# Half of k of batch 0 in fp32 from SyncE's queue, and three reorderings that go with it

## The chip, the cores and the metric

One core of one Trainium2 chip runs the whole program. The metric is the device time of one execution in microseconds (us), as the median of several executions. The profile's span, from the first to the last instruction, is about 1.75 us shorter than that time, so spans and times are not mixed below. Engines are called PE (TensorE), DVE (VectorE), ACT (ScalarE), POOL (GpSimd) and SP (SyncE).

## The reference

Linear attention in 8 batches of 8 heads, and then a gated feed-forward block on its output:

```python
def phi(x): return np.where(x > 0, x, np.exp(x) - 1.0) + 1.0     # = min(exp x, 1) + max(x, 0)
q_p, k_p = phi(q), phi(k)                       # q, k, v: [8, 8, 576, 64], fp32
kv  = einsum('bhsd,bhse->bhde', k_p, v)
z   = sum(k_p, axis=2)
num = einsum('bhsd,bhde->bhse', q_p, kv)
den = einsum('bhsd,bhd->bhs', q_p, z) + 1e-6
x   = (num / den) -> [4608, 512]
g   = x @ w_gate                                # [512, 1536]
out = (g * sigmoid(g) * (x @ w_val)) @ w_out    # [1536, 512]
```

## The kernel before

Tokens go through in 9 groups of 512. Layer 1 (`w_gate`, `w_val`, 12 blocks of columns) and layer 2 (`w_out`) are long matmuls of 512 columns in fp16, 216 ns each. Attention for the next batches is done in between, in short matmuls. Batch 0 and most of batch 1 are special: nothing precedes them that could hide their work. So for them q is transposed on PE, the denominators are made on PE ("corners" with Zr), and ACT takes 1/den as exp(-ln(den)).

All loads but one go through POOL's queue and are cast from fp32 to fp16 on the way. Half of q of batch 0 comes in fp32 from SP's queue and is cast by DVE:

```python
WARM = (34, 14, 16, 7, 3, 3, 2)        # dummy matmuls that keep PE busy during waits
...
nc.sync.dma_start(out=q32[:, :, :], in_=q[0]...[:, 0:2, :])
ld(q, qr, 0, 1)                        # cast load, second half of q of batch 0
ld2(k, kr, 0)                          # cast loads, both halves of k
ld(v, vr, 0, 0)
...
for l in range(2):
    nc.vector.tensor_copy(out=qr[0][:, l, :], in_=q32[:, l, :])
warm(WARM[0])
for lp in range(2):
    qtr(0, lp, pq[lp])                 # 16 transposes of q on PE
    warm(WARM[1 + lp])
    ph[lp][0]()                        # ACT: exp of q
exp_k(0, 0)                            # ACT: exp of k
exp_k(0, 1)
...
```

In layer 2 of group 0, the denominators of batch 1's tokens (`s4`) start at block 7 of 12, and `kv_corner(1, ...)` later writes k.v of batch 1 into the pair of PSUM banks `dz`:

```python
def lnrd(ps, i, w0=0, w1=512):
    for l2 in range(2):
        act(lnt[2 * i + l2][:, w0:w1], ps[l2][:, w0:w1], AF.Ln, bias=epsb[:, 0:1])
        act(rd[i][:, l2, w0:w1], lnt[2 * i + l2][:, w0:w1], AF.Exp, scale=-1.0)
...
step = {1: [s0], 3: [s1, s3], 7: [s4]}
FO = 8
for fb in range(FO):
    for f in step.get(fb, []): f()
    for t in range(4): l2_mm(0, t, fb)
for t in range(4):
    if t == 2:
        for lp in range(2): kv_corner(1, lp, kp, True, True)     # into dz
        r_copy(1, 0, 2, "VV")
    if t == 3: nx(0, dz)
    for fb in range(FO, FB): l2_mm(0, t, fb)
    if t < 3: l2_out(0, t, "V")
nx(1, cq)
```

In layer 2 of group 1, `block(1)` runs k.v of batches 2 and 3 (2 x 72 short matmuls) and 24 corner matmuls in one go.

## Time and profile before

| before | value |
|---|---|
| time, median (range) | 316.58 us (316.45 to 316.88, 4 executions) |
| span of the profiled execution | 315.4 us |
| PE busy | 309.3 us, 98% |
| first layer-1 matmul after blocks 0 and 1 (A) | 20.99 us |
| from A to the same point of group 1 (B) | 35.12 us |
| from B to the first layer-1 matmul of group 2 (C) | 30.21 us |
| from C to the end | 229.06 us |

The last four rows are read from the timeline of PE. They cut the span into four stretches: a change in the start shows in A, in layer 2 of group 0 in A to B, in the block of batch 2 in B to C.

The profile's chain of work that ended last (start us, duration us, what):

```profile
0.74 3.61 DMA q<-in_q_dram
...
4.38 1.14 DVE qr L425 x2
...
6.62 1.61 PE pp L122 x14
8.23 1.02 PE pp L368 x9
9.24 0.02 issue
9.27 1.02 ACT qT L118
10.29 1.06 ACT ek L118
11.35 0.02 issue
11.37 0.47 DVE ek L145
...
18.42 2.74 PE pp L274 x12
21.16 17.27 PE pp L290 x80
```

Up to 21 us several engines take turns, and L122 is dummy work. From there it is PE alone: 80 matmuls in 17.27 us, 216 ns each. Only the start has room. Note that the exp of k (ek) comes after the second exp of q (qT), which waits for a transpose of the second half of q.

The same start by windows (us, busy time of each engine with the number of its instructions, granted clock, DMA share, GB/s moved):

```profile
0.00:4.00 4.00, 2.94 (x28) 2.95 (x29) 0.89 (x7) 1.28 (x1) 2.87 (x9) 1.00 0.49 155
4.00:8.00 4.00, 3.62 (x39) 2.96 (x36) 1.42 (x3) 1.02 (x1) 3.50 (x6) 1.00 1.10 154
8.00:12.00 4.00, 3.83 (x55) 3.17 (x53) 2.78 (x6) 2.73 (x3) 2.18 (x3) 1.00 1.26 199
```

The bytes are counted as written, so a cast load counts half of what it reads. Between 4 and 8 us the queues move 154 GB/s, under the 199 of the next window: a hint that I did not use when I predicted. (The figure after the busy times is the granted clock. The view prints 1.00 there also where the trace has no clock record.)

Later, ACT and PE in layer 2 of group 0:

```profile
46.47 0.69 ACT L118 ACTIVATE lnt<-pp,epsb 128x512 f32<-128x512 f32 x1 [2.77 <-PE pp L252]
47.19 0.63 ACT L118 ACTIVATE rd<-lnt 128x512 f16<-128x512 f32 x1
47.72 0.67 ACT L118 ACTIVATE lnt<-pp,epsb 128x512 f32<-128x512 f32 x1
...
49.28 0.80 PE L183 MATMUL pp<-vr,kp 64*64 64x64 f16 x72
```

The second Ln ends at 48.39 us, and k.v of batch 1 starts 0.9 us later, at 49.28.

### The profile page before, as it was taken

What the parts mean: (1) busy time and instruction counts of PE and PEld (TensorE: products, weight loads), DVE (VectorE), ACT (ScalarE), POOL (GpSimd) and SP (SyncE); (2) the same over time, 40 slices, a digit from 0 to 9 for tenths busy, and PEclk for the clock granted to TensorE, in tenths of its full rate; (3) what the DMA queues carried; (4) which work ended last, traced back from release to release, by engine and by line L of the source; (5) the groups of instructions that cost most, each with busy time, mean ns of one, the idle gap of its engine ahead of it and who ended that gap; (6) DMA issues with size and microseconds to landing.
All of it is one profiled execution on the core that took longest, in us unless ns stands there. A gap on an engine that the chain in (4) does not pass through costs nothing.

```text
span 315.4 us, 5768 instructions
## 1 busy us (share of the span) xinstructions
PE 309.3 (98%) x2311; PEld 148.5 (47%) x2311; DVE 204.5 (65%) x354; ACT 151.2 (48%) x228; POOL 48.3 (15%) x73
## 2 busy tenths in 40 slices
PE   8999999999999999999999999999999999999994
PEld 7744444444544454445444544445444444444442
DVE  2754867999689676978598749874991434134410
ACT  2765849638653655357434743475331333133311
POOL 7655344300000230014000500000000000000000
PEclk9999999999999999999999999999999999999999
DMA  7999999997612297129803890314022400140014
GB/s 154 198 198 199 206 207 225 244 207 106 139 33 41 48 166 183 30 47 148 213 4 72 125 236 1 76 30 105 2 53 59 98 1 1 35 100 0 0 35 100
DMA packets 41163, 32.52 MB, mean 103 GB/s; under 512 B 16432, under 2 KB 36400, under 8 KB 41136
## 3 DMA queue, kind: packets, MB, share of 16 engines
q0 software_dynamic: 20736, 18.58, 37.9%
q1 hardware_dynamic: 20320, 13.54, 18.4%
q8 instruction: 18, 0.29, 0.4%
q14 instruction: 9, 0.07, 0.1%
q10 hardware_dynamic: 80, 0.03, 0.0%
HBM read 37.75 MB, written 9.44 MB: 150 GB/s over the span
## 4 chain that ended last, share of the span: by engine, by line
PE 96%; DMA 1%; DVE 1%; ACT 1%; issue 0%; DVEq 0%
PE pp L290 57%; PE pp L297 30%; PE pp L274 2%; PE pp L252 2%; PE pp L183 2%; DMA q<-in_q_dram 1%; PE pp L368 1%; PE pp L122 1%; DVE qr L425 0%; ACT ek L118 0%; ACT qT L118 0%; PE pp L393 0%; DVE xT L406 0%; PE pp L210 0%; DVE osb L320 0%
## 5 line engine op out<-in xcount | busy, mean ns | idle before, releaser
L118 ACT ACTIVATE sil<-pp 128x512 f16<-128x512 f32 x108 | 63.4, 597 | 102.0 <-PE pp L290 94.3
L290 PE MATMUL pp<-xT,wg 128*128 128x512 f16 x416 | 106.8, 379 | 0.0
L290 PE MATMUL pp<-xT,wv 128*128 128x512 f16 x416 | 106.8, 379 | 0.0
L283 DVE SCALAR_TENSOR_TENSOR hT<-pp,sil 128x512 f16<-128x512 f32 x108 | 72.2, 680 | 46.8 <-PE pp L290 34.9
L297 PE MATMUL pp<-wo,hT 128*128 128x512 f16 (+2 forms) x444 | 97.0, 374 | 0.6 <-DVE osb L320 0.6
L297 PEld LDWEIGHTS <-hT 128*128 128x128 f16 x444 | 41.9, 98 | 49.9 <-issue 2.1
L290 PEld LDWEIGHTS <-wv 128*128 128x128 f16 x416 | 40.6, 98 | 49.2
L290 PEld LDWEIGHTS <-wg 128*128 128x128 f16 x416 | 40.6, 98 | 48.5
L320 DVE TENSOR_SCALAR osb<-pp 128x512 f32<-128x512 f32 (+1 forms) x19 | 12.9, 681 | 32.7 <-PE pp L297 32.7
L118 ACT ACTIVATE osb<-pp 128x512 f32<-128x512 f32 (+1 forms) x18 | 10.2, 572 | 34.3 <-PE pp L297 34.3
L118 ACT ACT_TABLE_LOAD x13 | 16.7, 1283 | 2.3 <-PE pp L290 2.1
L118 ACT ACTIVATE ek<-kr 128x1152 f16<-128x1152 f16 x16 | 17.7, 1154 | 0.1
L657 POOL COPY gate<-qT 128x1 f16<-128x1 f16 x4 | 1.2, 305 | 97.9 <-DMA qT<-qp 70.2
L227 DVE TENSOR_TENSOR qp<-qp,rden 128x1152 f16<-128x1152 f16 x12 | 16.2, 1347 | 0.0
L218 DVE TENSOR_REDUCE den<-prod 128x18 f32<-128x1152 f16 x12 | 16.1, 1342 | 0.0
L269 DVE TENSOR_SCALAR xT<-pp 128x512 f16<-128x512 f32 (+1 forms) x14 | 8.8, 666 | 7.7 <-PE pp L252 7.7
L118 ACT ACTIVATE eq<-qr 128x1152 f16<-128x1152 f16 x12 | 13.2, 1147 | 0.0
L101 POOL DMA_DIRECT2D vr<-in_v_dram x16 | 11.7, 734 | 8.3 <-PE pp L290 3.1
L101 POOL DMA_DIRECT2D kr<-in_k_dram x16 | 11.5, 722 | 8.1 <-DMA vr<-in_v_dram 3.6
L101 POOL DMA_DIRECT2D qr<-in_q_dram x15 | 11.0, 734 | 7.2 <-DMA wo<-in_moe_w_out_dram 1.8
L145 DVE TENSOR_SCALAR ek<-ek 128x1152 f16<-128x1152 f16 x16 | 8.1, 508 | 5.7 <-ACT ek L118 5.7
L157 DVE TENSOR_TENSOR kp<-ek,kp 128x1152 f16<-128x1152 f16 x14 | 10.6, 758 | 0.5
(68 smaller groups left out, 189.5 us busy)
## 6 DMA issues: line engine op xcount, KB each, us to landing
out_dram<-osb SPq DMA_DIRECT2D x70, 128.0 KB, 3.7
kr<-in_k_dram POOLq DMA_DIRECT2D x16, 288.0 KB, 8.6
vr<-in_v_dram POOLq DMA_DIRECT2D x16, 288.0 KB, 9.9
qr<-in_q_dram POOLq DMA_DIRECT2D x15, 288.0 KB, 11.7
wo<-in_moe_w_out_dram POOLq DMA_DIRECT2D x3, 512.0 KB, 13.0
wg<-in_moe_w_gate_dram POOLq DMA_DIRECT2D x5, 256.0 KB, 9.7
wv<-in_moe_w_val_dram POOLq DMA_DIRECT2D x5, 256.0 KB, 10.3
q<-in_q_dram SPq DMA_DIRECT2D x1, 576.0 KB, 3.6
```

The costliest lines, as they stand in the source:

```text
L101: nc.gpsimd.dma_start(out=dst[b % NB][:, 2 * lp:2 * lp + 2, :], in_=src[b].rearrange("(l a) (c j) d -> (a c) l (j d)", a=2, j=J)[:, 2 * lp ...
L118: nc.scalar.activation(out=out, in_=in_, func=func, bias=bias, scale=scale)
L145: nc.vector.tensor_scalar(out=a, in0=a, scalar1=1.0, scalar2=None, op0=ALU.min)
L157: nc.vector.tensor_tensor(out=a, in0=ek[b % 2][:, lp, :, :], in1=a, op=ALU.add)
L183: nc.tensor.matmul(out=ps[hh][D * l2:D * l2 + D, D * lp:D * lp + D], lhsT=t[b % 2][rows, lp, j, D * l2:D * l2 + D], rhs=vr[b % NB][rows, 2 ...
L218: nc.vector.tensor_reduce(out=den[:, c, :], in_=prod[:, :, :].rearrange("p j (l d) -> p (j l) d", d=D), axis=AX.X, op=ALU.add)
L227: nc.vector.tensor_tensor(out=qv, in0=qv, in1=rden[:, c, :].unsqueeze(2).to_broadcast([P, 2 * J, D]), op=ALU.mult)
L269: nc.vector.tensor_scalar(out=dst, in0=ps[l2][:, c0:], scalar1=1.0 / SC, scalar2=None, op0=ALU.mult)
L283: nc.vector.scalar_tensor_tensor(out=hT[g % 2][:, fb, :], in0=ps[1][:, :], scalar=SC, in1=s[:, :], op0=ALU.mult, op1=ALU.mult)
L290: nc.tensor.matmul(out=ps[h][:, :], lhsT=w[:, c, P * fb:P * fb + P], rhs=xT[g % 2][:, c, :], start=(c == 0), stop=(c == 3))
L297: nc.tensor.matmul(out=l2p[(g, t)][:, n0:n1], lhsT=hT[g % 2][:, fb, P * t:P * t + P], rhs=wo[:, fb, n0:n1], start=(fb == 0), stop=(fb == F ...
L320: nc.vector.tensor_scalar(out=o[:, n0:n1], in0=ps[:, n0:n1], scalar1=1.0 / SC, scalar2=None, op0=ALU.mult)
```

## The change

It is meant to shorten the start: k's first half also comes in fp32 from SP, so it arrives without queueing behind q on POOL's queue, and its exp can run in ACT's gap between the two exps of q. One of the two casts of q moves to ACT. To relieve group 0, the second half of batch 1's k is processed later, and layer 2 of group 0 is laid out anew for that (FO 9, the denominators after the loop). k.v of batch 2 gets a place of its own. The dummies are cut. The core of the diff:

```diff
-    WARM = (34, 14, 16, 7, 3, 3, 2)
+    WARM = (32, 8, 8, 6, 3, 3)
@@ loads
-    nc.sync.dma_start(out=q32[:, :, :], in_=q[0]...)
+    for (src, dst) in ((q, q32), (k, k32)):
+        nc.sync.dma_start(out=dst[:, :, :], in_=src[0]...)
     ld(q, qr, 0, 1)
-    ld2(k, kr, 0)
-    ld(v, vr, 0, 0)
+    ld(k, kr, 0, 1)
+    ld2(v, vr, 0)
     ... (batch 1's k: its halves one and two weight loads later)
@@ batch 0
-    for l in range(2):
-        nc.vector.tensor_copy(out=qr[0][:, l, :], in_=q32[:, l, :])
+    nc.vector.tensor_copy(out=qr[0][:, 0, :], in_=q32[:, 0, :])
+    act(qr[0][:, 1, :], q32[:, 1, :])
     warm(WARM[0])
+    qtr(0, 0, pq[0])
+    ph[0][0]()
+    act(jl(ek, 0, 0), k32v, AF.Exp)
+    nc.vector.tensor_scalar(out=jl(kp, 0, 0), in0=k32v, scalar1=0.0, scalar2=None, op0=ALU.max)
     ... (cut: the same pieces of batch 0 in a new order)
@@ block(g), for batch 2
-            kv_all(b1)
-            r_copy(b1, 0, 2, "AA")
             kv_all(b2)
@@ layer2_0
-        step = {1: [s0], 3: [s1, s3], 7: [s4]}
-        FO = 8
+        step = {1: [s0], 4: [s1, s3], 5: [s5]}     # s0: now also batch 1's second k; s5: z
+        FO = 9
         for fb in range(FO):
             ...
+        s4()
@@ layer 2 of group 1
+                if t == 1 and g == 1:
+                    kv_all(b1)
+                    r_copy(b1, 0, 2, "AA")
```

More of the change, by code (lines that the diff above doesn't have):

```diff
@@ L65 @@
     q32 = sb.tile([P, 2, J * D], FP32, name="q32")
+    k32 = sb.tile([P, 2, J * D], FP32, name="k32")
     lnt = many([P, 512], FP32, "lnt", 4)
@@ L199, in r_copy, with zsum @@
                 nc.vector.tensor_copy(out=R[b % 3][:, l0:l1, hh, :], in_=src)
-    def zsum(b):
-        a = kp[b % 2]
-        nc.vector.tensor_tensor(out=zs[:, :, 0:4, :], in0=a[:, :, 0:4, :], in1=a[:, :, 4:8, :], op=ALU.add)
-        nc.vector.tensor_tensor(out=zs[:, :, 0:2, :], in0=zs[:, :, 0:2, :], in1=zs[:, :, 2:4, :], op=ALU.add)
-        nc.vector.tensor_tensor(out=zs[:, :, 0, :], in0=zs[:, :, 0, :], in1=zs[:, :, 1, :], op=ALU.add)
-        nc.vector.tensor_tensor(out=zs[:, :, 0, :], in0=zs[:, :, 0, :], in1=a[:, :, 8, :], op=ALU.add)
+    def zsum(b, l0=0, l1=2):
+        a, z = kp[b % 2][:, l0:l1, :, :], zs[:, l0:l1, :, :]
+        nc.vector.tensor_tensor(out=z[:, :, 0:4, :], in0=a[:, :, 0:4, :], in1=a[:, :, 4:8, :], op=ALU.add)
+        nc.vector.tensor_tensor(out=z[:, :, 0:2, :], in0=z[:, :, 0:2, :], in1=z[:, :, 2:4, :], op=ALU.add)
+        nc.vector.tensor_tensor(out=z[:, :, 0, :], in0=z[:, :, 0, :], in1=z[:, :, 1, :], op=ALU.add)
+        nc.vector.tensor_tensor(out=z[:, :, 0, :], in0=z[:, :, 0, :], in1=a[:, :, 8, :], op=ALU.add)
     def zb(b):
@@ L326, in l2_out @@
         return o
-    nc.sync.dma_start(out=q32[:, :, :],
-                      in_=q[0].rearrange("(l a) (c j) d -> (a c) l (j d)", a=2, j=J)[:, 0:2, :])
+    for (src, dst) in ((q, q32), (k, k32)):
+        nc.sync.dma_start(out=dst[:, :, :],
+                          in_=src[0].rearrange("(l a) (c j) d -> (a c) l (j d)", a=2, j=J)[:, 0:2, :])
     ld(q, qr, 0, 1)
     nc.gpsimd.iota(out=idx[:, :], pattern=[[-1, P]], base=0, channel_multiplier=1)
-    ld2(k, kr, 0)
-    ld(v, vr, 0, 0)
+    ld(k, kr, 0, 1)
+    ld2(v, vr, 0)
     ld_w1(0, 256, 0, 2)
-    ld(v, vr, 0, 1)
     ld_w1(0, 256, 2, 4)
@@ L340 @@
     ld_w1(512, 768)
+    ld_w1(768, 1024)
     ld(k, kr, 1, 0)
-    ld_w1(768, 1024)
-    ld(k, kr, 1, 1)
     ld_w1(1024, 1280)
     ld_w1(1280, 1536)
+    ld(k, kr, 1, 1)
     ld_w2(0, 4)
@@ L419, in t_add_half @@
                                        op0=ALU.max, op1=ALU.add)
+    k32v = k32[:, :, :].rearrange("p l (j d) -> p l j d", d=D)
     pq = pp4[0]
     kvp[0] = pp4[1]
+    X = [pp4[0][0], pp4[3][0]]
+    Y = [pp4[3][1], pp4[0][1]]
     ph = [t_phi_main(0, lp, pq[lp]) for lp in range(2)]
-    for l in range(2):
-        nc.vector.tensor_copy(out=qr[0][:, l, :], in_=q32[:, l, :])
+    nc.vector.tensor_copy(out=qr[0][:, 0, :], in_=q32[:, 0, :])
+    act(qr[0][:, 1, :], q32[:, 1, :])
     warm(WARM[0])
-    for lp in range(2):
-        qtr(0, lp, pq[lp])
-        warm(WARM[1 + lp])
-        ph[lp][0]()
-    exp_k(0, 0)
-    exp_k(0, 1)
+    qtr(0, 0, pq[0])
+    ph[0][0]()
+    act(jl(ek, 0, 0), k32v, AF.Exp)
+    nc.vector.tensor_scalar(out=jl(kp, 0, 0), in0=k32v, scalar1=0.0, scalar2=None, op0=ALU.max)
+    warm(WARM[1])
+    zt(0, 0, X[1], kp, True, False)
     ph[0][1]()
     ph[0][2]()
-    mx_k(0, 0)
-    zt(0, 0, pp4[3][0], kp, True, False)
+    warm(WARM[2], 2)
+    qtr(0, 1, pq[1])
+    ph[1][0]()
+    exp_k(0, 1)
+    mn_k(0, 0)
     warm(WARM[3], 2)
-    ph[1][1]()
-    mn_k(0, 0)
-    zt(0, 0, pp4[3][0], ek, False, True)
+    zt(0, 0, X[1], ek, False, True)
+    zr_copy(0, 0, X[1])
     mx_k(0, 1)
-    zr_copy(0, 0, pp4[3][0])
     warm(WARM[4], 2)
@@ L445 @@
     lnrd(pp4[2], 0)
-    zt(0, 1, pp4[3][1], kp, True, False)
+    ph[1][1]()
+    zt(0, 1, Y[0], kp, True, False)
+    t_add_half(1, pq[1], 0)
     mn_k(0, 1)
-    t_add_half(1, pq[1], 0)
     kv_corner(0, 0, kp, True, False)
     kv_corner(0, 0, ek, False, True)
-    zt(0, 1, pp4[3][1], ek, False, True)
+    zt(0, 1, Y[0], ek, False, True)
     r_copy(0, 0, 1, "VV")
     t_add_half(1, pq[1], 1)
-    zr_copy(0, 1, pp4[3][1])
-    warm(WARM[5], 2, pp4[1][1])
-    t_corners(0, R, 0, pp4[0])
-    x_t(0, 0, pp4[0], (0,))
-    t_corners(0, Zr, 1, pp4[3])
-    lnrd(pp4[3], 1)
-    x_t(0, 0, pp4[0], (1,))
-    warm(WARM[6], 2, pp4[1][1])
-    l1_mm(0, 0, pp4[2], (0,))
+    zr_copy(0, 1, Y[0])
+    t_corners(0, R, 0, X)
+    t_corners(0, Zr, 1, Y)
+    lnrd(Y, 1)
+    x_t(0, 0, X, (0,))
     kv_corner(0, 1, kp, True, False)
@@ L465 @@
     r_copy(0, 1, 2, "VV")
-    l1_mm(0, 1, pp4[0], (0,))
+    x_t(0, 0, X, (1,))
+    l1_mm(0, 0, pp4[2], (0,))
     t_corners(0, R, 1, pp4[1])
     x_t(0, 1, pp4[1])
-    for c in (1, 2, 3):
+    l1_mm(0, 0, pp4[2], (1,))
+    l1_mm(0, 1, X, (0, 1))
+    for c in (2, 3):
         l1_mm(0, 0, pp4[2], (c,))
-        l1_mm(0, 1, pp4[0], (c,))
+        l1_mm(0, 1, X, (c,))
     l1_post(0, 0, pp4[2])
-    l1_post(0, 1, pp4[0])
-    ring[:] = [pp4[3], pp4[1], pp4[2], pp4[0]]
+    l1_post(0, 1, X)
+    ring[:] = [Y, pp4[1], pp4[2], X]
     def none():
@@ L486, in p1_open @@
     def p1_open():
+        b1p["z"] = kvp[1] = pair()
+        ring.pop()
         b1p["q"] = pair()
@@ L490, in p1_z @@
     def p1_z():
-        b1p["z"] = kvp[1] = pair()
-        ring.pop()
         for lp in range(2):
-            ps = b1p["z"][0]
+            ps = b1p["z"][1]
             nc.tensor.matmul(out=ps[:, 2 * lp:2 * lp + 2], lhsT=zs[:, lp, 0, :], rhs=ob[:, 0:P:C],
@@ L503, in period0 @@
         b = 1
-        sl[6] = [lam(mx_k, b, 0), lam(exp_k, b, 0), lam(mx_k, b, 1), lam(exp_k, b, 1),
-                 lam(mn_k, b, 0), lam(add_k, b, 0), lam(mn_k, b, 1), lam(add_k, b, 1)]
-        sl[7] = [lam(zsum, b)]
+        sl[7] = [lam(mx_k, b, 0), lam(exp_k, b, 0), lam(mn_k, b, 0), lam(add_k, b, 0)]
+        sl[8] = [lam(zsum, b, 0, 1)]
+        sl[10] = [lam(mx_k, b, 1)]
         return sl
@@ L528, in block @@
             for lp in range(2):
-                if lp == 1:
-                    pair(kvp[b1])
-                    ring.insert(0, ring.pop())
                 num(b1, lp)
@@ L551, in layer2_0 @@
             l2_open(0, t)
-        p1_z()
         p1_open()
@@ L568, in s0 @@
             qtr(1, 0, cq[0])
-            for f in pm[0]:
-                f()
+            exp_k(1, 1)
+            pm[0][0]()
+            mn_k(1, 1)
+            add_k(1, 1)
+            zsum(1, 1, 2)
+            pm[0][1]()
+            pm[0][2]()
         def s1():
@@ L579, in s3, with s5 @@
             qtr(1, 1, cq[1])
-            for f in pm[1]:
-                f()
+            pm[1][0]()
+        def s5():
+            p1_z()
+            pm[1][1]()
+            pm[1][2]()
         def s4():
```

## The prediction

> What bounds the kernel now. The page's engine table has PE busy 98% of 315.4 us, and the chain that ended last is 96% PE. From 21.16 us on the chain is steady: 80 layer-1 matmuls take 17.27 us, 216 ns each, without idle. That can hardly shrink. The start can: the layer-1 matmuls of blocks 0 and 1 end at 21.16 us, though 16 x 0.216 = 3.5 us would do. Dummy matmuls fill the rest.
>
> The start, from the timelines: q in fp32 lands at 4.35; two DVE casts to 5.51; transposes; exp of q until 7.68; ACT idle until the second half of q (landed 7.59) is transposed, exp 9.27 to 10.29; only then exp of k to 11.35, min to 11.85, z sums, denominator corners 12.66; eight Ln/Exp on ACT from 13.11 to 18.4; the second denominators' corners at 15.37; last numerators at 18.01; then PE alone.
>
> What changes.
> 1. The second cast goes to ACT beside DVE's: ready about 5.1 instead of 5.51 (estimate, 0.65 us from ACT's 0.87 ns per element).
> 2. k's first half in fp32 from the SP queue: 590 KB, at the 0.4 MB/us that q reached 1.5 us, if the queue were alone. Casting loads land 1.43 us apart, the same read rate: no extra traffic, but k and the second half of q now share the engines. The Trainium skill (DMA: Bandwidth & Descriptors, Queues, rings and completion order) says each engine goes round robin between queues. Estimate: k at 6.5 to 7.3, second half of q at 8.5 to 9.2 (1 to 1.5 later), k's second half about 10, v by 13. No run shows it yet.
> 3. exp of k fills ACT's gap (7.3 to 8.4) instead of following the second exp of q. max of k reads fp32: VectorE: DVE Perf Modes, Mode 2x_2P, says fp32 single-source ops keep two elements per cycle; the trace's fp32 cast (459 ns for 576) agrees, so about 0.75 us against 0.45.
> 4. First denominator corners: about 11.5 (before 12.66). Ln/Exp from about 12.2 (before 13.11), since the second exps of q and k must still pass ACT first. Second denominators' corners 14.3 to 14.9 (before 15.37). PE then owes 4.7 us, plus small waits for xT: end of blocks 0 and 1 at 19.5 to 20.3 instead of 21.16. Critical gain 0.9 to 1.7 us of the 2 that exp of k gains; the second half of q gives back the rest.
> 5. Batch 1's second exp of k and z, later: off the path, 0. Weights land at the same times, needed 1 to 2 us sooner; slack is 2 us or more, except batch 1's second q (landed 40.8): a wait up to 0.3 us.
> 6. Layer 2 of group 0: denominators two steps later, so eight Ln/Exp (5.1 us) have 4.1 us of PE work over them instead of 6.1: group 1 may wait 0 to 0.4 us.
> 7. k.v of batch 2 alone: the block ran 2.26 us without PE idle: 0 to 0.1 us lost.
>
> Sum: 1.3 - 0.1 = about 1.2 us faster, 0.4%.
>
> Predicted 315.4 us, 8 in 10 between 314.4 and 316.3. Faster by over 2%: 0.01; within 2%: 0.98; slower: 0.01.
>
> What would show it: in DMA landings, k by 7.3 and q's half by 9.2; in ACT's timeline exp of k before the second exp of q; the first steady layer-1 matmul at 20 us or before; the distance from there to the end unchanged within 0.4 us.
>
> Wrong if: k lands after 8, q's half after 9.5 (then no gain), fp32 max runs at one element per cycle, fewer dummies lower PE's rate, or layer 2 of group 0 stalls by over 0.5 us.

## The result

| | before | after |
|---|---|---|
| time, median (range, executions) | 316.58 us (316.45 to 316.88, 4) | 315.31 us (315.28 to 315.36, 4) |
| ratio to before, 95% interval | | 0.9959 (0.9942 to 0.9976) |
| span | 315.4 | 313.6 |
| A | 20.99 | 18.60 |
| A to B | 35.12 | 35.85 |
| B to C | 30.21 | 30.07 |
| C to the end | 229.06 | 229.04 |

A ratio is the mean time of a kernel's fast runs over that of the other's fast runs of the same rounds, so it is not quite the ratio of the medians. The change is 1.3 us or 0.4% faster, and 315.31 lies on the predicted 315.4. The parts do not: the start gained 2.39 us in these two profiles where 0.9 to 1.7 was forecast, and layer 2 of group 0 lost 0.73. How much of the 2.39 us is the change's own is taken up under before_again.

The chain of the changed kernel:

```profile
1.27 4.65 DMA k<-in_k_dram
5.92 0.02 issue
5.94 0.77 DVE kp L434
...
7.15 0.90 PE pp L123 x8
8.05 0.57 PE pp L369 x16
...
13.37 0.12 PE pp L184 x14
13.49 0.37 issue
13.87 0.72 PE pp L184 x58
14.59 0.34 DVE R L200 x2
...
18.77 17.27 PE pp L291 x80
```

k lands at 1.27 + 4.65 = 5.92 us, earlier than any estimate of mine. The chain no longer waits for the second half of q. There is a new wait of 0.37 us in the middle of k.v, put down to "issue", that is, to nothing that the profile shows.

The windows of the same start:

```profile
0.00:4.00 4.00, 2.94 (x28) 2.94 (x29) 0.89 (x7) 1.28 (x1) 2.87 (x9) 1.00 0.51 172
4.00:8.00 4.00, 3.30 (x50) 2.38 (x47) 2.15 (x4) 2.76 (x3) 3.57 (x6) 1.00 1.15 262
8.00:12.00 4.00, 3.54 (x123) 2.64 (x123) 3.42 (x9) 3.31 (x5) 2.24 (x3) 1.00 1.26 203
```

The window from 4 to 8 us moves 262 GB/s where it moved 154. The half of q behind it landed at 7.70 us, against 7.59 before. So the fp32 load cost the cast loads 0.1 us here, and not the 1 to 1.5 us of the prediction (in the seven later fast profiles with the fp32 load, the half of q landed at 7.20 to 7.32 us, so not even that).

ACT and PE in layer 2 of group 0:

```profile
45.80 0.69 ACT L119 ACTIVATE lnt<-pp,epsb 128x512 f32<-128x512 f32 x1 [3.68 <-PE pp L253]
46.52 0.63 ACT L119 ACTIVATE rd<-lnt 128x512 f16<-128x512 f32 x1
47.06 0.67 ACT L119 ACTIVATE lnt<-pp,epsb 128x512 f32<-128x512 f32 x1
...
47.32 0.21 PE L184 MATMUL pp<-vr,kp 64*64 64x64 f16 x1
47.78 0.92 PE L184 MATMUL pp<-vr,kp 64*64 64x64 f16 x71 [0.25 <-ACT lnt L119]
```

The first matmul of k.v goes to the first bank of `dz` and runs; the second goes to the second bank, which the second Ln still reads until 47.73. It starts at 47.78.

### The profile page after: what moved, and what is told of

Same layout as the page of the kernel before. It is cut to its first block, busy times and chain, and to the rows that moved or that the text cites. A ratio compares the mean times of both kernels' runs of the same rounds, so it can differ in the third digit from the quotient of the medians.

```text
span 313.6 us, 5726 instructions
## 1 busy us (share of the span) xinstructions
PE 306.1 (98%) x2289; PEld 145.5 (46%) x2289; DVE 204.2 (65%) x357; ACT 151.7 (48%) x229; POOL 47.6 (15%) x72
## 4 chain that ended last, share of the span: by engine, by line
PE 94%; DVE 2%; DMA 1%; ACT 1%; issue 0%; SPq 0%
PE pp L291 57%; PE pp L298 30%; PE pp L275 2%; PE pp L184 2%; PE pp L253 2%; DMA k<-in_k_dram 1%; PE pp L123 1%; PE pp L369 1%; ACT lnt L119 0%; DVE qT L419 0%; DVE kp L434 0%; PE pp L211 0%; PE pp L394 0%; DVE xT L407 0%; DVE R L200 0%
## 5 line engine op out<-in xcount | busy, mean ns | idle before, releaser
L119 ACT ACTIVATE ek<-kr 128x1152 f16<-128x1152 f16 x15 | 16.8, 1156 | 0.1
L102 POOL DMA_DIRECT2D kr<-in_k_dram x15 | 10.8, 720 | 7.9 <-DMA vr<-in_v_dram 2.6
## 6 DMA issues: line engine op xcount, KB each, us to landing
qr<-in_q_dram POOLq DMA_DIRECT2D x15, 288.0 KB, 11.5
```

The lines of the kernel that those rows point to most:

```text
L102: nc.gpsimd.dma_start(out=dst[b % NB][:, 2 * lp:2 * lp + 2, :], in_=src[b].rearrange("(l a) (c j) d -> (a c) l (j d)", a=2, j=J)[:, 2 * lp ...
L119: nc.scalar.activation(out=out, in_=in_, func=func, bias=bias, scale=scale)
```

## The experiments

My theory after the result had three parts. The start gains because the fp32 load fills DMA time that was empty. The denominators, moved two blocks later, make k.v of batch 1 wait for its PSUM bank. Moving k.v of batch 2 is worth little. The third part fell. Twelve kernels were run, in three calls on three chips, each beside the kernel before; the ratios compare executions in the fast state alone.

| kernel | time, median | ratio to before (95%) | A | A to B | B to C |
|---|---|---|---|---|---|
| before_again | 316.33 | 0.9985 (0.9957 to 1.0013) | 19.98 | 35.12 | 30.21 |
| start_only | 318.47 | 1.0052 (1.0023 to 1.0080) | 18.60 | 35.12 | 32.24 |
| rest_only | 317.21 | 1.0003 (0.9980 to 1.0025) | 21.09 | 35.85 | 30.27 |
| kv_only | 316.20 | 0.9974 (0.9949 to 0.9999) | 21.74 | 35.11 | 30.08 |
| after_again | 315.57 (the five fast; 316.05 with the slow one) | 0.9983 (0.9963 to 1.0003) | slow | | |
| no_kv | 320.76 | 1.0138 (1.0117 to 1.0158) | 18.60 | 35.82 | 32.54 |
| ln_first | 315.25 | 0.9965 (0.9943 to 0.9986) | 18.85 | 35.41 | 30.07 |
| start_pad | 315.09 | 0.9959 (0.9942 to 0.9977) | 19.41 | 35.17 | 30.21 |
| k_by_pool | 318.35 | 1.0067 (1.0050 to 1.0084) | 21.55 | 35.72 | 30.12 |
| pad_early | 315.00 | 0.9961 (0.9949 to 0.9973) | 18.18 | 35.87 | 30.07 |
| best | 314.74 | 0.9958 (0.9946 to 0.9971) | 18.59 | 35.15 | 30.10 |
| best_pad | 314.51 | 0.9945 (0.9933 to 0.9956) | 18.38 | 35.15 | 30.18 |

The three stretches come from one profiled execution each; C to the end is 228.96 to 229.22 in all of them. The spread within A is large for starts as before (20.99, 19.98, 21.09 and 21.74 in four profiles). A to B repeats much better: 35.11 to 35.17 us with the old layer 2, 35.72 to 35.87 with the new one. So does B to C: 30.21 to 30.27 with the old block where PE does not stand, 30.07 to 30.18 with k.v of batch 2 moved. So the last two can rest on few profiles, and A needs profiles whose clocks are alike, as the next run shows.

### before_again: the kernel before, unchanged

> The kernel before, unchanged, for a second profile and the noise of the comparison. In the first profile of before the cast loads moved only about 290 GB/s at the source from 4 to 8 us, against 400 in the profile of after. If that is how this start always is, the second profile shows the same, blocks 0 and 1 end at 21.1 to 21.2 us and the span is 315.4. If the first profile was an unlucky start (its run took 317.15 us, over the median of 316.6), the second half of q lands earlier than 7.59 us or the span is nearer 314.9. Ratio 1.000.

A was 19.98 us, 1.0 earlier than in the first profile. The loads were not the reason: the half of q landed at 7.53 us against 7.59. The same 16 transposes of that half took 1.06 us in the first profile and 0.64 in this one:

```profile
8.16 1.06 PE L368 MATMUL pp<-id,qr 128*64 128x128 f16 x16
```

```profile
7.57 0.64 PE L368 MATMUL pp<-id,qr 128*64 128x128 f16 x16 [0.67 <-DMA qr<-in_q_dram]
```

The first fence is the timeline of the first profile of before, the second that of before_again. The Trainium skill (TensorE: Matmul & The Clock Gate, Part 1) says that PE's clock is released by a window of about 3.4 us that runs free of the kernel's start; the two rates at the same place agree with a clock released at different times. The kept traces settle it. Their first clock record begins at 10.24 us in the first profile and at 5.62 us in before_again: the slow transposes ran before it, the fast ones after it. (The window view's 1.00 for the time before is no record.) In all 13 fast profiles the second set of 16 transposes took 1.06 us where no record had begun or where the record says half clock, and 0.64 us elsewhere.

The record begins at 10.24, 5.62, 10.15 and 4.92 us in the four starts as before (before, before_again, rest_only, kv_only), and at 4.03 to 7.03 us in the nine others. So a good part of the 2.39 us is luck of the first profile: against before_again, whose clock came about as early as theirs and stayed, A is 1.38 us earlier in after, start_only and no_kv, 1.39 in best, 1.13 in ln_first, and 0.57 in start_pad (which stood 0.90 us in the issue wait that is treated below). Whether the new start also makes a late clock rarer (two of four against none of nine), these runs cannot tell.

### start_only, rest_only, kv_only: each part of the change alone

```diff
 start_only = the changed kernel, with p1_open, p1_z, period0, layer2_0, block(g)
 and the places of batch 1's k loads as before
 rest_only  = the kernel before + zsum in halves, p1_open, p1_z, period0, layer2_0,
 the places of batch 1's k loads as changed
 kv_only    = the kernel before + block(g) and the call at t == 1 as changed
```

> Only the start of the change (k in fp32 by SP, the new order of batch 0), with period 0, layer 2 of group 0 and the block of batch 2 as before. My theory: the start saves 2.4 us (blocks 0 and 1 end near 18.8) and after loses 0.75 of it again because its denominators' corners in layer 2 of group 0 come two steps later, so this one keeps the gain but for a wait of up to 0.3 us for batch 1's second q: stretch from the end of blocks 0 and 1 to the end of group 1's first layer-1 blocks 0.3 us or less over before's 35.1, time 314.2 to 314.8, faster than after. Rival: the loss in layer 2 comes from the earlier start itself (operands landing too late), then it is here too: stretch 35.7 or more, time 315.2 or more.

> Only the later second k and z of batch 1 and the layer 2 of group 0 of the change, with the start and the block of batch 2 as before. My theory: the wait of k.v of batch 1 for a Ln that still reads its PSUM bank comes here too: 0.5 to 0.8 us slower than before, 317.1 to 317.4. Rival (the loss belongs to the early start): 316.6, ratio 1.000.

> Only k.v of batch 2 moved out of the block before. From the two profiles group 1 is 0.14 us shorter in after; if that is the move, 316.45 here, ratio 0.9995; my prediction said 0 to 0.1 us slower. At the noise either way; the window of group 1 in the profile decides: 30.07 us (moved) or 30.21 (not).

The stretch A to B behaved as the theory said. It is 35.12 us with the old layer 2, whether the start is early (start_only) or late, and 35.85 with the new one, even behind the old start (rest_only). So the 0.73 us belong to the new layer 2, and the rival that blames the early start is out. rest_only's time of 317.21 was in my range, but its ratio of 1.0003 cannot show 0.7 us; the stretch can.

start_only missed its time by about 4 us (its profiled execution, the fastest of six, by 2). All of the miss that its profile shows is in B to C, in the block of batch 2, which this kernel has as before:

```profile
78.95 1.61 PE L184 MATMUL pp<-vr,kp 64*64 64x64 f16 x144
80.38 0.30 PE L253 MATMUL pp<-qT,Zr 64*64 64x128 f16 x8
80.50 0.40 PE L253 MATMUL pp<-qT,R 64*64 64x384 f16 x3
82.69 0.62 PE L253 MATMUL pp<-qT,R 64*64 64x384 f16 x13 [1.80 <-issue]
83.25 2.76 PE L298 MATMUL pp<-wo,hT 128*128 128x512 f16 x12
```

PE stands for 1.80 us between two corner matmuls of the same kind, waiting for nothing that the profile shows. The packet records have a packet of 16 KB on the queue marked instruction from 80.21 to 81.37 us. The Trainium skill (Runtime: NRT & Kernel Launch, Instruction fetch mechanics) says that an engine's instructions are streamed in blocks of 16 KiB, 256 instructions, and that crossing a block's end is mostly hidden. With matmuls of 216 ns, and a weight load for each, a block lasts 128 x 0.216 = 27.6 us (an estimate from the page's 256). In the block of batch 2, 168 matmuls with their weight loads, 336 instructions, pass in about 2 us. The theory I formed (the runs below call it the page theory, and a block a page): PE ran out of fetched instructions, because the start has 22 fewer dummies and the block boundary now falls into this burst.

kv_only shows 30.08 in B to C, 0.13 us less than before, as expected. Its time was 0.62 us under before's median of 316.82, with an interval up to 0.9999; one profile with a late start (A 21.74) says nothing on the rest of that. That start was late for two reasons: v landed at 12.89 in place of 11.90 us, and the granted clock was 0.50 from 15.16 to 18.57 us.

### after_again, no_kv, start_pad: the wait that nothing explains

```diff
 no_kv     = the changed kernel with block(g) as before (and without the call at t == 1)
 start_pad = start_only, and in l1():
-            for c in range(4):
-                nc.tensor.matmul(out=ps[h][:, :], ..., rhs=xT[g % 2][:, c, :], ...)
+            for (n0, n1) in (((0, 256), (256, 512)) if g == 0 and fb in (2, 3, 4) else ((0, 512),)):
+                for c in range(4):
+                    nc.tensor.matmul(out=ps[h][:, n0:n1], ..., rhs=xT[g % 2][:, c, n0:n1], ...)
```

> The changed kernel, unchanged, on this chip beside the others. Ratio to before 0.994 to 0.998, time 315.3 to 315.6. In the profile again: k lands by 6.0 us, q's half near 7.5, blocks 0 and 1 end near 18.8, a wait of k.v of batch 1 for Ln of about 0.25 us near 47.8, no wait over 0.5 us in the block of batch 2.

> The changed kernel with k.v of batch 2 put back into the block. start_only stood 1.80 us in that block, waiting for nothing that the profile shows, while a 16 KB packet of the instruction queue ran from 80.2 to 81.4 us. My new theory: 168 short matmuls in a row run PE out of fetched instructions when a page boundary falls there, and the start's 22 fewer dummies moved the boundary; moving k.v out is what protects against it. This kernel has as many PE instructions before the block as start_only, so it stands there too: a wait of 1 us or more at issue near 82 to 84 us, 316.5 or more, and more spread between runs than the changed kernel. Rival: moving k.v is worth the 0.14 us of the two profiles: 315.4 to 315.6, no wait.

> start_only with 24 of the layer-1 matmuls of group 0 in two halves of 256 columns: the same work, 24 more matmul and weight-load pairs before the block of batch 2, about the 22 that start_only lacks against before. Theory of the page boundary: the wait of 1.80 us in the block goes (under 0.3), time 314.4 to 315.0. Rival (the wait belongs to the data or the order of the start): it stays at 1 us or more, time as start_only, 317 to 318.5.

after_again's profile fell in a slow execution (402.0 us at a granted clock of 0.756), and it is not used. Its five fast executions gave 315.49 to 317.21 us with a median of 315.57, and the gain on this chip is smaller, 0.9983. The two highest, 316.53 and 317.21, have a granted clock of 0.993 on record, the other three 0.997 to 0.999.

no_kv is the changed kernel with only that one part undone. It stood 1.95 us at the same place and took 320.76 us, 1.4% slower than before:

```profile
81.41 0.34 PE L253 MATMUL pp<-qT,R 64*64 64x384 f16 x3
83.70 0.62 PE L253 MATMUL pp<-qT,R 64*64 64x384 f16 x13 [1.95 <-issue]
```

start_pad does the same work as start_only with 24 more pairs of weight load and matmul ahead of the block, and no data, order or wait of the block is touched. The wait is gone:

```profile
79.82 1.62 PE L184 MATMUL pp<-vr,kp 64*64 64x64 f16 x144
81.26 0.32 PE L253 MATMUL pp<-qT,Zr 64*64 64x128 f16 x8
81.43 0.73 PE L253 MATMUL pp<-qT,R 64*64 64x384 f16 x16
```

B to C is back at 30.21, and the time is 315.09 in place of 318.47 (on another chip). So the wait there depends on how many instructions come before, which is the page theory's forecast and not that of a wait for data. The instruction packets moved with it: the packet that ran at 80.21 in start_only ran at 76.08 here, before the burst. In every case seen, PE goes on 1.25 to 1.51 us after the packet's last byte (82.69 after 81.37, 83.70 after 82.19, 13.87 after 12.52).

A count of the instructions in the kept traces leaves little room for another cause. The queue marked instruction has the same line in the page of every kernel but for the share of time (packets, MB, share; here from start_pad):

```profile
q8 instruction: 18, 0.29, 0.3%
```

That is 18 packets of 16 KB for 2,289 to 2,313 matmuls with as many weight loads: 18 x 256 = 4,608 instructions, where 4,578 to 4,626 were run. And every issue wait of PE over 0.1 us stands before the same matmul, counted from the start of the program: before the 224th (start_only, after, no_kv, ln_first, best, start_pad, and the slow profile of after_again) or before the 864th (start_only and no_kv). Between these lie 640 matmuls and their weight loads, 1,280 instructions, 5 x 256. So the waits are at the ends of blocks. In start_pad the 864th matmul falls into the burst too, at 81.13 us, but the packet had ended at 77.23, and PE did not stand. What counts is whether the next block has come by then.

Moving k.v of batch 2 cuts one burst of 168 matmuls into 72 and 96, and with it no profile of a fast execution shows the wait there. The profiled wait of no_kv is 1.95 us, while its other four executions were 319.95 to 321.61 against the profiled 317.78; that the wait is longer in those was not seen. But the clock of each is on record: 0.998 in the profiled one, 0.992 in the next two, 0.988 and 0.987 in the last two. One stretch at half clock as in kv_only, 3.41 us long, takes 0.005 off the mean (an estimate: 0.5 x 3.41 / 316) and up to 1.7 us of PE's work. So these executions look like the profiled one with one or two such stretches; four of start_only's (0.992 and 0.993) do too. That the wait brings them on is not shown; k_by_pool, below, has such a stretch right after a wait of 2.24 us.

### ln_first, best: the PSUM bank

```diff
 ln_first: the changed kernel, in layer2_0
         def den(lp, ps):
             t_corners(1, Zr, lp, ps)
-            lnrd(ps, lp)
+            for l2 in range(2):
+                act(lnt[2 * lp + l2][:, :], ps[l2][:, :], AF.Ln, bias=epsb[:, 0:1])
+            for l2 in range(2):
+                act(rd[lp][:, l2, :], lnt[2 * lp + l2][:, :], AF.Exp, scale=-1.0)
 best: ln_first, and
             if t == 3:
                 nx(0, dz)
+                l2_out(0, 2, "V")
             ...
-            if t < 3:
+            if t < 2:
                 l2_out(0, t, "V")
```

> The changed kernel, with the two Ln of each denominator pair before its two Exp in layer 2 of group 0. My theory: k.v of batch 1 waits for the second Ln of the bank pair it writes; the Ln now ends 0.6 us sooner, the wait of 0.25 us before k.v and its slow start go: group 0's layer 2 period 18.1 us in place of 18.6, time 0.4 to 0.5 us under the changed kernel. Rival (the loss is the later denominators as such, by xT for group 1): period unchanged or longer.

> The changed kernel with the Ln before the Exp in layer 2 of group 0 (as in ln_first) and the third output copy after the first xT of group 1: the wait of 0.16 us of group 1's first layer-1 matmuls goes too. Period of group 0's layer 2 17.95 to 18.0 us, where ln_first has 18.14; time 314.7 to 315.0, ratio to before 0.994 to 0.996.

```profile
46.06 1.27 ACT L119 ACTIVATE lnt<-pp,epsb 128x512 f32<-128x512 f32 x2 [3.69 <-PE pp L253]
47.72 0.80 PE L184 MATMUL pp<-vr,kp 64*64 64x64 f16 x72
```

(the timeline of ln_first). With both Ln first, the bank is free 1.27 us after the first Ln starts, where it took 1.93 (45.80 to 47.73) in after. PE's wait of 0.25 us for the Ln is gone from the timeline, and A to B fell from 35.85 to 35.41. best takes the rest: the third output copy no longer stands on DVE ahead of the first xT of group 1, and A to B is 35.15 us, within 0.03 of before's 35.12. Together that is 0.70 of the 0.73 us: 0.44 with the bank free sooner, 0.26 with the copy out of xT's way. ln_first's time, 315.25, is 0.3 under the 315.57 of after_again's fast executions in the same rounds (where 0.4 to 0.5 was expected; the intervals overlap widely).

### k_by_pool: does the route of k matter, or the order?

```diff
 the changed kernel, and
-    for (src, dst) in ((q, q32), (k, k32)):
+    for (src, dst) in ((q, q32),):
+    ld(k, kr, 0, 0)
     ld(q, qr, 0, 1)
-    act(jl(ek, 0, 0), k32v, AF.Exp)
-    nc.vector.tensor_scalar(out=jl(kp, 0, 0), in0=k32v, ..., op0=ALU.max)
+    exp_k(0, 0)
+    mx_k(0, 0)
```

> The changed kernel with its whole new order, but k's first half as a casting load, first in POOL's queue, as q's half and the rest follow. Theory (the fp32 load by SP fills DMA time that stands empty while the cast queue starts up): k lands near 7.6 us and every load behind it 1.4 us later than in the changed kernel, q's half near 9.0; from 4 to 8 us the DMA queues move 150 to 170 GB/s in place of about 260; blocks 0 and 1 end at 19.6 to 20.4. Rival (the order of work gives the gain, and the route of k is worth little): 18.8 to 19.2, time within 0.3 us of the changed kernel's 315.3 to 315.6.

The route is what counts. k landed at 8.04 us, the half of q at 9.47, and the windows moved

```profile
4.00:8.00 4.00, 2.17 (x31) 1.64 (x28) 0.61 (x2) 1.71 (x2) 3.34 (x5) 1.00 1.02 133
8.00:12.00 4.00, 3.42 (x35) 2.37 (x36) 2.59 (x4) 1.42 (x2) 2.03 (x3) 0.60 1.20 201
```

133 GB/s from 4 to 8 us. A was 21.55, later than I expected (19.6 to 20.4). Part of that is this kernel's own: PE stood 2.24 us for k, and its granted clock fell to 0.60 in the next window, so its transposes took 1.06 us again. The clock record says 0.50 from 8.84 to 12.25 us. That can cost half of these 3.41 us at most, 1.7 us (an estimate); without it A would still be about 19.8, 1.2 us after the changed kernel's, and the rival had 18.8 to 19.2. The size is thus not clean; the landings and the GB/s are.

Reckoned at the source, where a cast load reads twice what it writes, and by the ends of the packets, the five profiles of kernels without the fp32 k moved 259 to 313 GB/s from 4.0 to 7.5 us, and the eight fast ones with it 398 to 409. In all of them the first cast packet runs just when SP's loads drain: at 3.5 to 3.6 us without the fp32 k, at 4.97 to 5.13 with it, though POOL issued that load at 1.2 us. (SP's last packets end at 3.8 to 4.0 and at 5.5 to 5.6 us.) So the cast queue starts behind SP's, and it then reaches its full rate at once if SP's second load lasted until 5 us. Why it takes until about 8 us to reach that rate otherwise stays open; no run separates it.

### pad_early, best_pad: using the page theory

```diff
-    WARM = (32, 8, 8, 6, 3, 3)
+    WARM = (35, 12, 12, 6, 3, 3)
     ...
-    warm(WARM[2], 2)
+    warm(WARM[2])
 best_pad = best with these
```

> The changed kernel with 11 more dummy matmuls in the first 8 us, where PE waits anyway, and none after. The page theory: PE crosses into its next instruction page about 0.5 us sooner, so the wait at issue before k.v of the second half (0.37 to 0.9 us near 13.9) shrinks by 0.3 us or more, and blocks 0 and 1 end 0.2 to 0.5 us sooner: 18.3 to 18.6, time 0.2 to 0.5 under the changed kernel. Rival (that wait is set by when the page comes through the full DMA queues, whatever PE has done): wait and time unchanged.

> best and pad_early together. If both theories hold, 314.3 to 314.8, ratio 0.993 to 0.9955; if the pad does nothing, as best.

The second site of an issue wait is the start itself, in k.v of batch 0: 0.37 us in the profile of after, 0.12 in start_only, 0.44 in ln_first, 0.52 in no_kv, 0.54 in best, 0.90 in start_pad. Eleven more dummies, in time that PE spends waiting anyway, make PE cross into its next block of instructions sooner. The first instruction packet ended at 12.06 us in pad_early and 12.03 in best_pad, in place of 12.52 in after, and the wait is gone:

```profile
13.48 0.51 PE L184 MATMUL pp<-vr,kp 64*64 64x64 f16 x36
13.81 0.49 PE L184 MATMUL pp<-vr,ek 64*64 64x64 f16 x36
14.22 0.39 PE L275 MATMUL pp<-xT,wg 128*128 128x512 f16 x1
```

(the timeline of best_pad). A is 18.18 in pad_early and 18.38 in best_pad, against 18.60 and 18.59 in after and best. More dummy work made the kernel faster. best_pad is at 314.51 us, 0.9945 of before, the lowest of all kernels here; best, in the same rounds, is at 314.74. Its interval (0.9933 to 0.9956) overlaps that of the changed kernel's first comparison (0.9942 to 0.9976), which was on another chip, so that it beats the changed kernel rests on the stretches as much as on the times.

## Why the prediction was right or wrong

The number was right: 315.31 against 315.4, and 0.4% was forecast. That it hit so well is in part luck. Errors cancelled, and with clocks alike the stretches add up to 1.38 - 0.73 + 0.14 = 0.8 us, where the first comparison's medians differ by 1.27 and those of after_again's rounds (315.57 against 316.45) by 0.9. The rest of the 1.27 stays open; late clocks in some executions of the kernel before, as in its first profile (317.15 us), are possible.

1. q ready at 5.1 us: right; ACT's cast ended at 5.17, and the transposes of DVE's half started at 5.00.
2. "k at 6.5 to 7.3, second half of q at 8.5 to 9.2 (1 to 1.5 later)": this step failed. k landed at 5.92 and q's half at 7.70. The two queues do not share from the start; the cast queue waits until SP's loads drain, and the time after that was a quarter to a third unused before (259 to 313 of some 400 GB/s). k's 590 KB were almost free, as k_by_pool and the 398 to 409 GB/s with it show.
3. max of fp32 in about 0.75 us: right, 0.76 (the prediction's 459 ns is one of the two fp32 casts in the trace; the other took 752). exp of k in ACT's gap: right, at 6.81.
4. Gain of the start 0.9 to 1.7 us: right in size where the clocks are alike, 1.38 us against before_again, the one old start with such a clock; the 2.39 us between the two first profiles has the first profile's late clock in it. But the way there was not the one forecast. By the failed step the first denominators' corners came at 9.98 and not 11.5, 1.67 us before before_again's 11.65. Part of that was lost again, 0.37 us of it in the issue wait that I had not foreseen.
5. A wait for batch 1's second q: none came.
6. Layer 2 of group 0, 0 to 0.4 us: mis-sized, 0.73. The xT wait that I named was there (0.16 us). What I missed was larger: the bank of `dz` that k.v of batch 1 writes and the Ln still reads. I had counted when the results of the Ln are needed, and not when their source has to be free. The prediction had named a stall of over 0.5 us in this layer as a sign that it was wrong; this sign came.
7. k.v of batch 2, "0 to 0.1 us lost": wrong in sign, 0.14 us gained, and wrong in kind. I read it as a shuffle of work without idle time. In the changed kernel it is what keeps PE from running out of instructions, and taking it out cost 5.2 us of median time against after_again's fast executions in the same rounds (320.76 against 315.57), 1.95 of which a profile shows.

The prediction's own test, that the distance from the first steady matmul to the end is unchanged within 0.4 us, failed: it grew by 0.57 (35.85 + 30.07 + 229.04 against 35.12 + 30.21 + 229.06).

## What to carry to other kernels

Count instructions as well as time: a burst of short matmuls can outrun the instruction fetch, the wait shows only as "issue" in the middle of a group of equal instructions, and it moves when any earlier part gains or loses instructions, even dummies. Two profiles of one kernel can differ by 1 us because the clock was granted at different times, so compare starts only where the clock records are alike. When consumers of a PSUM bank are moved later, look for who writes that bank next. And before costing a transfer by fair sharing, look at what the queues really move in that window: empty time early in a kernel can make an extra load nearly free.

## What the Trainium skill lacked or had wrong

- DMA: Bandwidth & Descriptors, Queues, rings and completion order, says each engine goes round robin between the queues that have work. Here the cast loads, issued at 1.2 us, moved their first packet at 3.5 to 3.6 us when SP had one load and at 4.97 to 5.13 when it had two: behind all but the last half microsecond of SP's loads, not between them. (The traces do not show when the descriptors of a cast load reach the engines; that they were ready by 3.5 us in both cases is inferred.) No page has the slow rise of the cast queue after that (259 to 313 GB/s at the source from 4.0 to 7.5 us, 398 to 409 when SP's second load precedes it).
- Runtime: NRT & Kernel Launch, Instruction fetch mechanics, calls the crossing of a 16 KiB block mostly hidden. In bursts of short matmuls it cost 1.80 and 1.95 us in one place and 0.12 to 0.90 in another, and PE went on only 1.25 to 1.51 us after the packet's end. The page gives no way to see it coming; here a count of matmuls and weight loads did (every wait before matmul 224 or 864, 5 x 256 instructions apart).
- TensorE: Matmul & The Clock Gate, Part 1: the free-running window agrees with two rates for the same transposes (1.06 and 0.64 us for 16). The page warns that clock events in a trace can be unreliable; here they agreed with the rate of these transposes in all 13 fast profiles. The 1.00 in the window view before the first record (up to 10.24 us in before) is no such event.
